# Tiles 6 to 15 of x loaded already turned, and centred by an accumulating DMA

## The chip, the cores and the metric

The kernel runs on one core of one Trainium2 chip. Its engines are TensorE (PE; its weight loads are listed as PEld), VectorE (DVE), ScalarE (ACT), GpSimd (POOL) and SyncE (SP). SP, ACT and POOL also issue DMA transfers, and each issues its own in the order of its queue. The metric is device time in microseconds; the kernel before was timed three times, and the median counts.

## The reference

All arrays are fp32. x has 2048 rows of 512. The two branches, a linear attention with 32 heads of 16 and a gated MLP of width 1376, both read the layer-normalised x.

```python
xn = _layernorm(x, axis=-1)                       # (x - mean) / sqrt(var + 1e-5)
return x + _A_ref(xn, wqkv, w_phi, wo) + _B_ref(xn, w_in, w_sp, b_sp, w_out)

# A: q, k, v = split(xn @ wqkv);  phi(t) = [softmax(t @ w_phi), softmax(-t @ w_phi)] per head
#    kv = phi_k^T v;  z = sum_s phi_k;  o = (phi_q kv) / (phi_q z + 1e-6);  A = o @ wo
# B: z = gelu(xn @ w_in);  z1, z2 = halves of z;  z2 = layernorm(z2)
#    g = w_sp @ z2 + b_sp;  B = (z1 * g) @ w_out
```

## The kernel before

The 2048 rows are cut into 16 tiles of 128 rows (`NT`), the 512 columns into 4 chunks of 128 (`ND`). Each matmul is made of three in fp32r, with operands cut into a rounded high part and a rest (`mm3`, lines 54 to 57): high by high, high by low, low by high. The high part is written by ACT (`round_h`, L47), the rest by VectorE (`rest_l`, L51).

There are three stages. The first, up to about 210 us, goes over the 16 tiles of x and makes q, k, v, their softmaxes, the sum of k and v, and the first half of the MLP's input product. The second makes the second half, and the third, the longest, the product with `w_sp` by a scheme of seven products; at its end the outputs are put together.

The change is in the first stage. TensorE contracts over partitions, so it needs x with its columns on partitions, x^T. For each tile s, `centered(s)` does this, called two tiles ahead, at step s - 2 of the loop in line 451:

- SP loads the rows, 256 KB (`load_x`, L179); five buffers (`XB`) hold them.
- VectorE makes mean and variance (`stats`, L260 and L261); POOL makes the negative mean (`neg_mean`, L265), and 1 / sqrt(var + eps) (L92, L93), which is applied later, to the outputs of the projections.
- ACT adds the negative mean to each row, in place (`center`, L269).
- TensorE turns the tile by four matmuls with the identity into one PSUM buffer (`transposed`, L275). Four such buffers (tag `mm`) are shared with the projections of q, k and v.
- ACT and VectorE split the PSUM buffer into high part and rest (`split_x`, L47 and L51) in a tile of the pool `xz`. That is x^T of the tile, named `xT` in the profile, kept for all later products.

A step s of the loop then fetches the rows of tile s + 4, projects k and makes its pair of softmaxes (`softmax_pair`: L111, L112, L117 and L118 on VectorE, the exponential L119 on ACT, the sums L122 and reciprocals L123 on VectorE), calls `centered(s + 2)`, projects some q, whose softmaxes go to DRAM (`e_d`, a POOL transfer), adds the normalised k softmaxes into `zacc` by an accumulating POOL transfer (`add_kv`, L307 and L308) and multiplies them with v in batches (L319), projects v of tile s + 1, and makes z1 of older tiles (`z1_raw`, L149).

The pool `xz` has 16 buffers. Before the x^T tiles need them all, they hold raw weights, and six of these (`spare`, line 449) serve as the softmax tiles of steps 2, 3, 4, 5, 8 and 9.

The order on each engine isn't the order of the text: a planner simulates the kernel by its own costs, and each engine's instructions are written out in the order in which they became ready there, earlier text first. `tc.issue_after(ins)` puts the instructions of its block behind `ins` on the engine of `ins`. Once it is written out, the order on each engine and queue is fixed, and an instruction that waits holds up all that stand behind it.

Of the kernel before, what the change touches and what calls it, by code (L numbers as in the profile page):

```python
# [10 lines left out]
F32 = mybir.dt.float32  # L11
F32R = mybir.dt.float32r
AF = mybir.ActivationFunctionType
ALU = mybir.AluOpType
# [4 lines left out]
P = 128  # L19
S, D, H, DH, FH = 2048, 512, 32, 16, 688  # L20
NT = S // P
ND = D // P
FC = FH // 2
NG = 4
NF = 2 * D
# [4 lines left out]
EPS_LN = 1e-5  # L30
EPS_DEN = 1e-6
XB = 5
NP = NT // 2
HP, QP = P // 2, P // 4
FP = 3 * P
# [4 lines left out]
def mixer(ctx: ExitStack, tc: tile.TileContext, x, x_t, wv, wqkT, phi_bd, wo, w_in, wst, b_r, w_out, out):  # L40
    nc = tc.nc
    pe, act, dve, pool, sp = nc.tensor, nc.scalar, nc.vector, nc.gpsimd, nc.sync


    def round_h(eng, h, src):
        if eng is act:
            return act.activation(h, src, AF.Copy).ins  # L47
        return eng.tensor_copy(h, src).ins

    def rest_l(l, src, h, eng=None):  # L50
        return (eng or dve).tensor_tensor(l, src, h.bitcast(F32), op=ALU.subtract).ins  # L51
# [18 lines left out]
    def xz_tile(n, dt, name):  # L70
        return xz.tile([P, SL], dt, tag="xz", name=name)[:, :n]

    mid = ctx.enter_context(ExitStack())
    dram = ctx.enter_context(tc.tile_pool(name="dram", bufs=1, space=DRAM))
# [2 lines left out]
    u_d = dram.tile([NT, FU, P], F32, name="u_d")  # L77
    kvT_d = dram.tile([P, D], F32, name="kvT_d")
    zb_d = dram.tile([P, NF], F32, name="zb_d")

    ident = cst.tile([P, P], F32, name="ident")
    make_identity(nc, ident)
# [3 lines left out]
    mv_x = cst.tile([P, NT, 2], F32, name="mv_x")  # L86
    r_x = cst.tile([P, NT], F32, name="r_x")

    def rstd_of(mv, r, stats=None):
        if stats is not None:  # L90
            dve.bn_aggr(mv, stats)
        pool.tensor_scalar_add(mv[:, 1:2], mv[:, 1:2], EPS_LN)  # L92
        pool.tensor_tensor(r, mv[:, 1:2], mhalf, op=ALU.pow)  # L93

    def heads(ap):
        return ap.rearrange("p (h d) -> p h d", d=DH)
# [8 lines left out]
    def bc(ap, n):  # L105
        return ap.unsqueeze(2).to_broadcast([P, n, DH])

    def softmax_pair(pl, src, tag, scale=1.0, ebufs=2, meanwhile=lambda: None, er=None):

        mm = pl.tile([P, 2, H], F32, tag=tag + "mm", bufs=1, name="mm")  # L110
        dve.tensor_reduce(mm[:, 0], heads(src), axis=AX.X, op=ALU.max)  # L111
        dve.tensor_reduce(mm[:, 1], heads(src), axis=AX.X, op=ALU.min)  # L112
        if er is None:
            er = pl.tile([P, NF + 2 * H], F32, tag=tag + "e", bufs=ebufs, name="e")
        e, r = er[:, :NF], er[:, NF:]
        e2 = e.rearrange("p (h a d) -> p h a d", a=2, d=DH)
        dve.tensor_tensor(e2[:, :, 0], heads(src), bc(mm[:, 0], H), op=ALU.subtract)  # L117
        dve.tensor_tensor(e2[:, :, 1], bc(mm[:, 1], H), heads(src), op=ALU.subtract)  # L118
        act.activation(e, e, AF.Exp, scale=scale)  # L119
        meanwhile()  # L120
        sm = pl.tile([P, 2 * H], F32, tag=tag + "sm", bufs=1, name="sm")
        dve.tensor_reduce(sm, heads(e), axis=AX.X, op=ALU.add)  # L122
        dve.reciprocal(r, sm)  # L123
        return er
# [47 lines left out]
    with ExitStack() as p0:  # L172
        res = p0.enter_context(left("p0res", 1))
        wk = p0.enter_context(left("p0wk", 2))
        ps = p0.enter_context(psum("p0ps", 4))

        def load_x(s):
            t = wk.tile([P, D], F32, tag="x", bufs=XB, name="xt")
            sp.dma_start(t, x[s * P:(s + 1) * P, :])  # L179
            return t  # L180
# [5 lines left out]
        def stage(name, dt=F32):  # L186
            return xz_tile(2 * FH, dt, name).rearrange("p (a b) -> p a b", a=2)
# [6 lines left out]
        bd_t = stage("bd")  # L194
# [50 lines left out]
        xt, v, rounded, ready = {}, {}, [], []  # L245

        def fetch(s):
            if s < NT:
                xt[s] = load_x(s)

        def split_x(src):
            t = xz_tile(2 * D, F32R, "xT").rearrange("p (a b) -> p a b", a=2)
            xT.append(t)
            src = src.rearrange("p a b -> p (a b)")
            rounded.append(round_h(act, t[:, 0], src))
            return rounded[-1], rest_l(t[:, 1], src, t[:, 0])

        def stats(s, keep=lambda **ins: None):
            st6 = wk.tile([P, 6], F32, tag="st6", name="st6")
            dve.bn_stats(st6, xt[s])  # L260
            keep(dve=dve.bn_aggr(mv_x[:, s], st6).ins)  # L261

        def neg_mean(s):
            nm = wk.tile([P, 1], F32, tag="nm", name="nm")
            pool.tensor_scalar_mul(nm, mv_x[:, s, 0:1], -1.0)  # L265
            return nm

        def center(s, nm):
            return act.activation(xt[s], xt[s], AF.Identity, bias=nm).ins  # L269

        def transposed(s):
            xs = xt.pop(s)
            pt = ps.tile([P, ND, P], F32, tag="mm", name="pt")
            for c in range(ND):
                ins = pe.transpose(pt[:, c], xs[:, c * P:(c + 1) * P], ident).ins  # L275
            return pt, ins

        def centered(s):
            stats(s)
            nm = neg_mean(s)  # L280
            rstd_of(mv_x[:, s], r_x[:, s:s + 1])
            with tc.issue_after(rounded[s - 2]):
                center(s, nm)
            split_x(transposed(s)[0])

        def keep_v(s, p):
            v[s] = wk.tile([P, D], F32, tag="v", bufs=4, name="v")
# [6 lines left out]
        spare = {}  # L294

        def proj_k(s):
            er = spare[s].rearrange("p a b -> p (a b)")[:, :NF + 2 * H] if s in spare else None
            return softmax_pair(wk, proj(s, wqk_h[:, 1], wqk_l[:, 1]), "k", r_x[:, s:s + 1], er=er)

        def proj_q(s):  # L300
# [28 lines left out]
        wkT_t = load_rows.raw  # L329
        fetch(2)  # L330
        wqT = load_rows(wqkT[:D])
        wqT_t = load_rows.raw
        fetch(3)
        w1r = [stage("w1row") for _ in range(2)]
# [5 lines left out]
        def keep(**ins):  # L340
            for i in ins.values():
                queue.enter_context(tc.issue_after(i))
# [6 lines left out]
            keep(pe=i)  # L349

        queue = ExitStack()
        tbl = wk.tile([P, 1], F32, tag="nm", name="tbl")
        keep(act=act.activation(tbl, mhalf, AF.Identity, bias=mhalf).ins)
        warm_up(7)
        stats(0, keep)
# [4 lines left out]
        nm = neg_mean(1)  # L360
# [17 lines left out]
        t = xz_tile(2 * D, F32R, "xT").rearrange("p (a b) -> p a b", a=2)  # L378
# [8 lines left out]
        for cs, pt in zip(halves, pts):  # L387
            src = pt.rearrange("p a b -> p (a b)")
# [8 lines left out]
        p = ps.tile([P, D], F32, tag="mm", name="proj")  # L397
        proj(0, wv_h, wv_l, p, (0, 1, 2))
        keep(pe=proj.last)
        pt = turned(1)  # L400
# [4 lines left out]
        p = ps.tile([P, D], F32, tag="mm", name="proj")  # L405
# [12 lines left out]
        nm = settled(2)  # L418
# [4 lines left out]
        nm = settled(3)  # L423
        p = ps.tile([P, D], F32, tag="mm", name="proj")
        proj(0, wqk_h[:, 1], wqk_l[:, 1], p, (0, 1))
        keep(pe=proj.last)
        pt = turned(2)
# [18 lines left out]
        split_x(turned(3))  # L446
        z1_raw(wk, za, 0, 2)
        keep(pe=zproj.last)
        spare.update(zip((2, 3, 4, 5, 8, 9), [bd_t] + wkT_t + wqT_t[:1] + w1r))
        n1, nq = 1, 0  # L450
        for s in range(NT):
            fetch(s + 4)
            er = ek[s] if s < len(ek) else proj_k(s)
            if 1 < s < NT - 2:
                centered(s + 2)
            while nq < (s - 2) * NT // (NT - 3):
                proj_q(nq)
                nq += 1
            add_kv(s, er)
            if s == 0:  # L460
                tiles = fold_tiles(((za, "z"), (ps, "mm")))
                keep(pe=fold(0, wqT, tiles))
                folded(0, tiles)
            elif s == 1:
                proj_v(3)
            elif 2 < s < NT - 1:
                proj_v(s + 1)
            while n1 < s * (NT - LAG) // (NT - 1):
                z1_raw(wk, za, n1, 2)
                n1 += 1  # L470
            if s == 3:
                queue.close()
# [33 lines left out]
    NQ = NT // QC  # L506
    NC = NP * NQ


    SEQ = [(i, q) for i in range(NP) for q in (range(NQ) if i < NP - 1 else (1, 2, 3, 0))]  # L510

# [40 lines left out]
    with ExitStack() as p1:  # L552
# [44 lines left out]
        for s in range(NE):  # L597
            et = load_q(s, tb.tile([P, QW], F32, name="et") if s else tmp1.tile([P, 4, D], F32, tag="zhl", name="et").rearrange("p a b -> p (a b)")[:, :QW])
            tmp = zw.tile([P, 4, FC], F32, tag="z2", bufs=2, name="qtmp").rearrange("p a b -> p (a b)")[:, :NF]
            e, _ = q_fin(et, tmp, zb)  # L600
# [57 lines left out]
    for s in range(NT):  # L658
        p = zproj((kv_ps_p, zc, zbp, za)[s % 4], s, w2, (0, 1) if s % 2 == 0 else (1, 0))
# [7 lines left out]
        for k, q in p:  # L667
            ins = act.activation(z[:, k], q, AF.Gelu_apprx_tanh, scale=r_x[:, s:s + 1]).ins
# [67 lines left out]
    def gate(i, cb, z, u, ut, after=None):  # L736
# [10 lines left out]
        def turn():  # L747
# [3 lines left out]
            for b in range(0, P, BL):  # L751
                (pool if i == NP - 2 else sp).dma_start(dst[:, :, b:b + BL], src[b:b + BL].rearrange("p (m b) -> p m b", b=BL))

# [49 lines left out]
    for n in range(NC):  # L803
        i = SEQ[n][0]
        if n % NQ == 1 and i < NP - 1:
            z = load_z1(i)
        products(n, g)
        if n % NQ == NQ - 1 and i < NP - 1:
            c = gt.tile([P, 2, FU], F32, tag="c", name="c")
# [5 lines left out]
        if n + 2 < NC:  # L815
            A[n + 2] = prep_a(n + 2, raw.pop(n + 2))
        if n % NQ == NQ - 1 and i < NP - 1:
            turn = gate(i, cb, z, c, z, prep_a.last)
# [12 lines left out]
        if n == NC - 2:  # L831
            es[0], es[1] = first_q(0), first_q(1)
            t = xz_tile((KF + 1) * P, F32R, "u1")
# [10 lines left out]
    wk = ctx.enter_context(left("cwk", 2))  # L844
# [125 lines left out]
    p, nxt = {}, dict(enumerate(uT))  # L970
# [61 lines left out]
```

## Time and profile before

| | |
|---|---|
| Three runs | 627.75, 628.66, 630.17 us; median 628.66 us |
| The profiled execution | 627.78 us |
| Its span, first to last instruction | 626.1 us |
| Granted TensorE clock | 0.999 |
| Transposes of x tiles after the first | 60, mean 272 ns |
| Centring passes on ACT | 15, median 712 ns |
| Statistics passes on VectorE | 16, median 688 ns |
| Busy, of the span | PE 99%, PEld 90%, DVE 81%, ACT 45%, POOL 17% |
| DMA | 98.40 MB, mean 157 GB/s |

A row of the profile names engine, line of the kernel, operation, and what is written from what (`pt<-ident,xt` writes `pt` from `ident` and `xt`); then how many, the busy microseconds and the mean duration in nanoseconds, or minimum, median and maximum. In a timeline the first column is the start and the second how long the row's instructions took together. A row of waits says who waited for whom: microseconds in total, how often, and the longest. Matmuls overlap, so the sum of their durations is more than the time that they take.

### The profile page before, as it was taken

To read this page: it belongs to the slowest core of one execution; us is meant where nothing else is said; L and a number is where in the kernel's file an instruction comes from. 1 tells how busy PE (TensorE), PEld (TensorE's weight loads), DVE (VectorE), ACT (ScalarE), POOL (GpSimd) and SP (SyncE) were. 2 spreads that over 40 slices of the span, in tenths; PEclk is the share of its full clock that TensorE was granted. 3 is DMA by queue.
4 is the path that set the end of the run, shared out by engine and by line. 5 is a ranking of instruction groups with operands and counts; after the bars stand their busy time and mean duration, and the time that the engine had idled before them with its cause. 6 is when DMAs were issued, how large, how long until landed. Compare 5 with 4: busy or idle time off the path is not lost.

```text
span 626.1 us, 11429 instructions
## 1 busy us (share of the span) xinstructions
PE 619.1 (99%) x4406; PEld 565.3 (90%) x4406; DVE 508.8 (81%) x893; ACT 280.7 (45%) x446; POOL 104.8 (17%) x187
## 2 busy tenths in 40 slices
PE   8999999999999999999999999999999999999996
PEld 7888888888888999999999999999999877788775
DVE  5999998987988398989898897696978899989211
ACT  5653434443333367877434444243445433334331
POOL 4142122111011015442000000000000212211110
PEclk9999999999999999999999999999999999999999
DMA  9445465354336868001454845637367799984722
GB/s 313 164 109 144 121 156 155 88 143 136 104 93 173 274 234 285 2 2 35 147 115 147 193 96 153 136 119 175 88 174 232 224 297 330 320 249 97 180 34 51
DMA packets 87590, 98.40 MB, mean 157 GB/s; under 512 B 46560, under 2 KB 59616, under 8 KB 87296
## 3 DMA queue, kind: packets, MB, share of 16 engines
q1 hardware_dynamic: 75200, 58.12, 32.4%
q0 software_dynamic: 10032, 33.92, 20.7%
q10 hardware_dynamic: 2304, 5.64, 2.4%
q8 instruction: 34, 0.56, 0.4%
q14 instruction: 20, 0.16, 0.1%
HBM read 56.37 MB, written 30.54 MB: 139 GB/s over the span
## 4 chain that ended last, share of the span: by engine, by line
PE 98%; DVE 0%; ACT 0%; POOL 0%; issue 0%; DVEq 0%; POOLq 0%
PE g L57 11%; PE g L56 11%; PE g L55 11%; PE proj L57 7%; PE proj L55 7%; PE proj L56 7%; PE zps L57 6%; PE zps L55 6%; PE zps L56 6%; PE pout L55 5%; PE pout L57 5%; PE pout L56 5%; PE ptq L890 1%; PE po L905 1%; PE kvps L319 1%; PE pout L919 1%
## 5 line engine op out<-in xcount | busy, mean ns | idle before, releaser
L56 PE MATMUL g<-B,A 128*128 128x344 f32 x448 | 143.3, 320 | 0.0
L55 PE MATMUL g<-B,A 128*128 128x344 f32 x448 | 142.8, 319 | 0.0
L57 PE MATMUL g<-B,A 128*128 128x344 f32 x448 | 140.6, 321 | 0.1
L55 PEld LDWEIGHTS g<-B,A 128*128 128x128 f32 x448 | 84.3, 188 | 0.0
L56 PEld LDWEIGHTS g<-B,A 128*128 128x128 f32 x448 | 84.2, 188 | 0.0
L57 PEld LDWEIGHTS g<-B,A 128*128 128x128 f32 x448 | 83.6, 188 | 0.4 <-DVE A L51 0.4
L47 ACT ACTIVATE A<-S 128x512 fp32r<-128x512 f32 x64 | 39.4, 630 | 71.3 <-DVE S L542 51.3
L55 PE MATMUL proj<-wqk_h,xT 128*128 128x512 f32 x128 | 50.6, 395 | 0.0
L57 PE MATMUL proj<-wqk_h,xT 128*128 128x512 f32 x128 | 50.2, 393 | 0.0
L56 PE MATMUL proj<-wqk_l,xT 128*128 128x512 f32 x128 | 49.9, 390 | 0.0
L47 ACT ACTIVATE A<-wf 128x512 fp32r<-128x512 f32 (+1 forms) x64 | 33.2, 521 | 36.3 <-DMA wf<-in_wst 14.3
L119 ACT ACTIVATE e<-e,r_x 128x1024 f32<-128x1024 f32 x26 | 29.9, 1150 | 40.2 <-DVE e L118 39.6
L51 DVE TENSOR_TENSOR A<-S,A 128x512 fp32r<-128x512 f32 x64 | 43.1, 686 | 4.8 <-ACT A L47 4.3
L55 PE MATMUL zps<-w_0h,xT 128*128 128x344 f32 x128 | 41.4, 323 | 0.0
L57 PE MATMUL zps<-w_0h,xT 128*128 128x344 f32 x128 | 41.0, 320 | 0.0
L55 PE MATMUL zps<-w_1h,xT 128*128 128x344 f32 x128 | 40.9, 320 | 0.0
L57 PE MATMUL zps<-w_1h,xT 128*128 128x344 f32 x128 | 40.7, 319 | 0.0
L56 PE MATMUL zps<-w_0l,xT 128*128 128x344 f32 x128 | 40.6, 317 | 0.0
L56 PE MATMUL zps<-w_1l,xT 128*128 128x344 f32 x128 | 40.6, 317 | 0.0
L51 DVE TENSOR_TENSOR A<-wf,A 128x512 fp32r<-128x512 f32 (+1 forms) x64 | 35.0, 549 | 2.6 <-ACT A L47 2.4
L707 POOL DMA_DIRECT2D z1t<-z_d x16 | 8.7, 547 | 165.5 <-DMA u_d<-z1t 98.7
L122 DVE TENSOR_REDUCE sm<-e 128x64 f32<-128x1024 f32 x26 | 31.4, 1207 | 5.1 <-ACT e L119 5.0
(205 smaller groups left out, 1432.7 us busy)
## 6 DMA issues: line engine op xcount, KB each, us to landing
wf<-in_wst SPq DMA_DIRECT2D x64, 256.0 KB, 3.4
e_d<-e POOLq DMA_DIRECT2D x16, 544.0 KB, 4.6
et<-e_d SPq DMA_DIRECT2D x16, 544.0 KB, 6.4
er<-et POOLq DMA_DIRECT2D x12, 512.0 KB, 6.4
z_d<-z1f ACTq DMA_DIRECT2D x16, 344.0 KB, 2.6
z1t<-z_d POOLq DMA_DIRECT2D x16, 344.0 KB, 5.2
zacc<-e POOLq DMA_DIRECT2D x10, 512.0 KB, 4.7
u<-u_d SPq DMA_DIRECT2D x15, 320.0 KB, 5.6
```

The source lines that it names most:

```text
L47: return act.activation(h, src, AF.Copy).ins
L51: return (eng or dve).tensor_tensor(l, src, h.bitcast(F32), op=ALU.subtract).ins
L55: pe.matmul(dst, ah, bh, start=start, stop=False)
L56: pe.matmul(dst, ah, bl, start=False, stop=False)
L57: return pe.matmul(dst, al, bh, start=False, stop=stop).ins
L119: act.activation(e, e, AF.Exp, scale=scale)
L122: dve.tensor_reduce(sm, heads(e), axis=AX.X, op=ALU.add)
L319: i = pe.matmul(kv_acc[k:k + QP, m // 4], vs[:, m * QP:(m + 1) * QP], e[:, m * HP:(m + 1) * HP], start=first and m < 4 and len(ready) == n ...
L707: pool.dma_start(t[:, k, :FH], z1_d[2 * i + k])
L890: pe.transpose(pt[:, a, k].bitcast(F32R), src, ident_r)
L905: lasts[3] = pe.matmul(po[r][c * QP:(c + 1) * QP, k], kvT[rows, m // 2, cols], fs[m // 4][rows, m // 2 % 2], start=True, stop=True).ins
L919: lasts[2] = pe.matmul(p, rt, w, start=False, stop=i == NT - 1 and k == 1).ins
```

## The change

From tile 6 on (`FT`), x^T no longer comes from TensorE. The kernel already had `x_t` among its inputs, x with each tile turned, and did not use it. Now:

- `fetch` still loads the rows of each tile, as before up to tile 5, and six steps ahead from tile 6 on, for the statistics alone.
- `lay_x(s)`, four steps ahead, loads the turned tile, again 256 KB, on SP. Tiles 6 to 12 lie two by two in buffers of `xz`, tiles 13 to 15 (`LT`) in the buffers of the row tiles.
- `send_mean(s)`, four steps ahead and on VectorE behind the last split, makes the statistics, the negative mean on POOL and 1 / sqrt(var + eps), and SP stores the negative means to DRAM (`nm_d`), four copies of 128 numbers, each number a piece of its own.
- `center_t(s)`, three steps ahead and on POOL's queue behind the next tile's negative mean, is one POOL transfer that adds these 512 numbers to each of the 128 rows of the turned tile.
- `split_x` reads the turned tile from SBUF, behind the step's k softmax differences on VectorE and its exponential on ACT.

The four transposes and the centring pass of tiles 6 to 15 are gone. Steps 8 and 9 take fresh buffers of `xz` for their softmax tiles in place of raw weight tiles. The small tiles `nm` have four buffers in place of two.

```diff
+FT, LT = 6, 13
+    nm_d = dram.tile([NT, ND, P], F32, name="nm_d")
-        dve.tensor_tensor(e2[:, :, 1], bc(mm[:, 1], H), heads(src), op=ALU.subtract)
-        act.activation(e, e, AF.Exp, scale=scale)
+        less = dve.tensor_tensor(e2[:, :, 1], bc(mm[:, 1], H), heads(src), op=ALU.subtract).ins
+        softmax_pair.last = less, act.activation(e, e, AF.Exp, scale=scale).ins
...
-            nm = wk.tile([P, 1], F32, tag="nm", name="nm")
+            nm = wk.tile([P, 1], F32, tag="nm", bufs=4, name="nm")
...
+        lay = {}
+        def lay_x(s):
+            if s >= LT:
+                xc = wk.tile([P, D], F32, tag="x", bufs=XB, name="xt")
+            elif (s - FT) % 2 == 0:
+                lay_x.pair = xz_tile(2 * D, F32, "xc")
+                xc = lay_x.pair[:, :D]
+            else:
+                xc = lay_x.pair[:, D:]
+            sp.dma_start(xc, x_t[s].rearrange("p c t -> p (c t)"))
+            lay[s] = xc
+        def send_mean(s):
+            with tc.issue_after(split_x.last):
+                stats(s)
+            xt.pop(s)
+            nm = wk.tile([P, 1], F32, tag="nm", bufs=4, name="nmt")
+            send_mean.last = pool.tensor_scalar_mul(nm, mv_x[:, s, 0:1], -1.0).ins
+            sp.dma_start(nm_d[s].rearrange("c t -> t c"), nm.to_broadcast([P, ND]))
+            rstd_of(mv_x[:, s], r_x[:, s:s + 1])
+        def center_t(s):
+            with tc.issue_after(send_mean.last):
+                pool.dma_start(lay[s], nm_d[s].rearrange("c t -> (c t)").unsqueeze(0).to_broadcast([P, D]), accum_op=ALU.add)
...
-            er = spare[s].rearrange("p a b -> p (a b)")[:, :NF + 2 * H] if s in spare else None
+            er = (spare[s] or stage("er")).rearrange("p a b -> p (a b)")[:, :NF + 2 * H] if s in spare else None
...
-        spare.update(zip((2, 3, 4, 5, 8, 9), [bd_t] + wkT_t + wqT_t[:1] + w1r))
+        spare.update(zip((2, 3, 4, 5, 8, 9), [bd_t] + wkT_t + wqT_t[:1] + [None] * 2))
...
-            fetch(s + 4)
+            if s + 4 < FT:
+                fetch(s + 4)
+            if FT <= s + 6 < NT:
+                fetch(s + 6)
+            if FT <= s + 4 < NT:
+                lay_x(s + 4)
             er = ek[s] if s < len(ek) else proj_k(s)
-            if 1 < s < NT - 2:
+            if 1 < s < FT - 2:
                 centered(s + 2)
+            elif FT - 2 <= s < NT - 2:
+                with tc.issue_after(softmax_pair.last[0]), tc.issue_after(softmax_pair.last[1]):
+                    split_x(lay.pop(s + 2))
+            if FT <= s + 4 < NT:
+                send_mean(s + 4)
+            if FT <= s + 3 < NT:
+                center_t(s + 3)
```

More of the change, by code (lines that the diff above doesn't have):

```diff
@@ L253, in split_x @@
             xT.append(t)
-            src = src.rearrange("p a b -> p (a b)")
             rounded.append(round_h(act, t[:, 0], src))
-            return rounded[-1], rest_l(t[:, 1], src, t[:, 0])
+            split_x.last = rest_l(t[:, 1], src, t[:, 0])
+            return rounded[-1], split_x.last
         def stats(s, keep=lambda **ins: None):
@@ L275, in transposed @@
                 ins = pe.transpose(pt[:, c], xs[:, c * P:(c + 1) * P], ident).ins
-            return pt, ins
+            return pt.rearrange("p a b -> p (a b)"), ins
         def centered(s):
@@ L351, in mixer @@
         queue = ExitStack()
-        tbl = wk.tile([P, 1], F32, tag="nm", name="tbl")
+        tbl = wk.tile([P, 1], F32, tag="nm", bufs=4, name="tbl")
         keep(act=act.activation(tbl, mhalf, AF.Identity, bias=mhalf).ins)
```

## The prediction

> **What bounds the kernel now.** I read the page first, its busy shares and its chain of waits, then the waits of TensorE alone.
>
> ```profile
> span 626.1 us, 11429 instructions
> ...
> PE 619.1 (99%) x4406; PEld 565.3 (90%) x4406; DVE 508.8 (81%) x893; ACT 280.7 (45%) x446; POOL 104.8 (17%) x187
> ...
> PE 98%; DVE 0%; ACT 0%; POOL 0%; issue 0%; DVEq 0%; POOLq 0%
> ```
> ```profile
> PE idle L348 <- POOL ident masks.py:199: 1.8, 1, 1.8
> ```
>
> The chain that ends last is TensorE from one end to the other, and TensorE waited once in the whole span: 1.8 us for the identity at the start. So the time is the sum of what TensorE is given, and a microsecond taken from its stream comes off the end, if nothing else becomes late. The edit lies in the first stage, the loop over the 16 tiles. There the second thing to read is VectorE, by stretches of 20 us (the columns are the stretch, its length, then busy time and count of PE, weight loads, DVE, ACT and POOL).
>
> ```profile
> 45.00:65.00 20.00, 20.00 (x216) 17.06 (x216) 19.81 (x32) 6.92 (x9) 5.93 (x12) 1.00 0.46 115
> 65.00:85.00 20.00, 20.00 (x104) 17.39 (x103) 18.75 (x31) 9.79 (x13) 4.50 (x10) 1.00 0.57 153
> 85.00:105.00 20.00, 20.00 (x105) 17.48 (x105) 18.35 (x28) 7.87 (x11) 4.03 (x7) 1.00 0.42 117
> 105.00:125.00 20.00, 20.00 (x216) 16.95 (x215) 18.01 (x28) 8.23 (x12) 3.42 (x7) 1.00 0.48 137
> 125.00:145.00 20.00, 20.00 (x102) 17.23 (x101) 17.77 (x26) 8.15 (x11) 2.85 (x4) 1.00 0.51 144
> ```
>
> TensorE is full in every stretch; VectorE is full up to 65 us (19.81 of 20) and has 1.25 to 2.2 us left in each later one. ACT and POOL have more than half their time free. VectorE is therefore the engine that the change must not load.
>
> **What is removed, and its price.** Tiles 6 to 15 lose four transposes each, 40 in all, and one centring pass each on ACT. A transpose's own duration says little, because matmuls overlap; the price is read from starts. Around the transposes of tile 9:
>
> ```profile
> 88.08 0.40 PE L57 MATMUL proj<-wqk_h,xT 128*128 128x512 f32 x1
> 88.31 0.60 PE L275 MATMUL pt<-ident,xt 128*128 128x128 f32 x4
> 88.67 0.48 PE L55 MATMUL proj<-wqk_h,xT 128*128 128x512 f32 x1
> ...
> 91.28 0.39 PE L57 MATMUL proj<-wqk_h,xT 128*128 128x512 f32 x1
> ...
> 94.00 0.39 PE L57 MATMUL proj<-wqk_h,xT 128*128 128x512 f32 x1
> ```
>
> From 88.08 to 91.28 lie twelve projection matmuls and the four transposes: 3.20 us. From 91.28 to 94.00 lie twelve of the same matmuls alone: 2.72 us. The four transposes cost 3.20 - 2.72 = 0.48 us: 0.36 from their first start to the next matmul's, and 0.12 in matmuls spaced wider behind them. Ten tiles give 4.8 us. The lower bound takes the 0.36 alone, 3.6 us; the upper takes the whole 0.60 for which the group is shown busy, 6.0 us. I take 4.8, since it is a difference of two equal pieces of work.
>
> The Trainium skill (TensorE: Matmul & The Clock Gate, Part 4: PE-mode transpose) gives some 275 ns for a transpose in one kernel's context. An estimate that adds this up 40 times would be 11.0 us, a median of 617.7. The starts above contradict the adding: four of them pass in 0.36 us here, so the page's figure is a latency and not a cost.
>
> **What ACT and VectorE do per tile.** ACT loses its centring (0.71 us each, 7.1 us in all, of an engine under half busy: worth nothing to the end). The split into high and low part now reads SBUF where it read PSUM:
>
> ```profile
> L269 ACT ACTIVATE xt<-xt,nm x15: 707/712/724, 8.7 to 140.0; 128x512 f32<-128x512 f32 x15
> L51 DVE TENSOR_TENSOR xT<-pt,xT x17: 417/681/693, 6.1 to 167.4; 128x512 fp32r<-128x512 f32 x15, 128x256 fp32r<-128x256 f32 x2
> L51 DVE TENSOR_TENSOR A<-S,A 128x512 fp32r<-128x512 f32 x64 | 43.1, 686 | 4.8 <-ACT A L47 4.3
> ```
>
> The last row is the same subtraction from SBUF in the third stage: 686 ns against 681, no difference. The statistics (one pass and a small one) stay, but move. Now they run as soon as a row tile has landed; in the changed kernel those of tile s+4 stand behind the split of tile s+2.
>
> ```profile
> 31.03 1.22 DVE L260 BATCH_NORM_STATS2 st<-xt 128x6 f32<-128x512 f32 x2
> ...
> 58.46 0.69 DVE L260 BATCH_NORM_STATS2 st<-xt 128x6 f32<-128x512 f32 x1
> ```
> ```profile
> L261 DVE BATCH_NORM_AGGREGATE mv_x<-st 128x2 f32<-128x6 f32 x6 | 1.0, 166 | 0.0
> ```
>
> Counting the passes from the first tile on, the two at 31.03 are tiles 6 and 7 and the one at 58.46 is tile 11. Behind the splits, 66 us sees only tile 8 done. So three passes of 0.69 + 0.17 = 0.86 us, 2.6 us, leave the stretch in which VectorE is full and go into the stretch from 65 to 145. There VectorE has 18.75 + 18.35 + 18.01 + 17.77 = 72.9 us; with them 75.5. TensorE's 80 us shrink by seven tiles to 80 - 7 x 0.48 = 76.6. VectorE still fits, by 1.1 us, and it enters the stretch 2.6 us less late than now. Also the transposed tile no longer takes one of the four PSUM buffers that the projections share, which gives TensorE more room when VectorE is late. I cost the move at nothing; the cover is thin, and without it the first rival comes.
>
> **What is added.** Per tile: a second load of 256 KB on SP, POOL's small product with -1 (in place of the one before), a store of the negative means on SP (512 single numbers), and one accumulating transfer from POOL, 256 KB. No accumulating transfer from DRAM into SBUF is in the trace. The nearest rows are the sums into `zacc`, same queue and stage, 512 KB, and the stores of `e_d`; for the scattered store, `u_d`, which goes in 128-byte pieces.
>
> ```profile
> L308 POOL DMA_DIRECT2D zacc<-e x10: 864/878/1072, 34.0 to 199.9; - x10
> DMA to landing us min/median/max: 4.5/4.6/6.7
> ```
> ```profile
> DMA to landing us min/median/max: 2.8/5.1/10.7
> ```
> ```profile
> u_d<-z1t SPq DMA_DIRECT2D x24, 184.0 KB, 4.4
> xt<-in_x SPq DMA_DIRECT2D x16, 256.0 KB, 3.9
> ```
>
> The first landing row is that of `zacc`, the second that of `e_d`, its reloads among them. I take 4.6 us for the centring transfer, bounded by 2.8 and 10.7. The load has a step and more (the tiles' distance, 12.5 us, worked out below) for its 3.9 us, and the store one step for its 4.4. POOL spends 0.88 us on issuing each centring, 9 us in all, against a load of 4 us in 20. Queued behind SP's wait for the means are only later loads, which are asked for two steps ahead; behind POOL's wait stand the next `zacc` and `e_d` transfers. What is tight is the way from one split to the next (rows of POOL's product, of the split of tile 7 on VectorE, of that of tile 8 on ACT):
>
> ```profile
> L265 POOL TENSOR_SCALAR nm<-mv_x x15: 210/239/250, 6.0 to 117.9; 128x1 f32<-128x1 f32 x15
> ```
> ```profile
> 68.58 0.68 DVE L51 TENSOR_TENSOR xT<-pt,xT 128x512 fp32r<-128x512 f32 x1
> ```
> ```profile
> 76.61 0.60 ACT L47 ACTIVATE xT<-pt 128x512 fp32r<-128x512 f32 x1 [1.45 <-PE pt L275]
> ```
>
> The split of tile 7 ends at 69.26; then come the statistics (0.86), POOL's product (0.24, taken as 0.3 with its start) and, behind it, the transfer that centres tile 8: it starts at about 70.6 and lands at 75.2. ACT now begins tile 8's split at 76.61. It fits by 1.4 us, in the tightest of the steps that I followed. So the added work lies beside TensorE, and its cost is 0.
>
> **Sum.** 626.1 - 4.8 = 621.3 us of span; the profiled execution took 627.78, 1.7 us more than its span, so 623.0. The median of the runs, 628.66, lies 0.9 above that execution: 623.9. By the bounds 3.6 and 6.0: 625.1 and 622.7.
>
> **Rivals.** First, VectorE becomes the pace in the stretch from 65 to 145 us. Its idle time there is 80 - 72.9 = 7.1 us; the waits of VectorE between 45 and 145 us name most of it:
>
> ```profile
> DVE st L260 <- DMA xt<-in_x: 2.6, 2, 1.9
> DVE sm L122 <- ACT e L119: 2.3, 3, 1.2
> ```
>
> The 2.6 for row tiles goes, as these are fetched a step or two earlier. If the other 4.5 stays as it is, VectorE needs 75.5 + 4.5 = 80.0 us, the stretch stays 80 long, and only the three tiles outside it (6, 14, 15) pay: 3 x 0.48 = 1.4, 627.2 us. For it: the 1.1 us margin, and an order that the planner writes out anew and that may fit the chip less well. Against: TensorE never waited for VectorE, even where that was busy 19.81 of 20.
>
> Second, slower: centring is a loop. A tile's transfer is issued behind the statistics of a tile that stand behind the split of the tile before, and its landing releases the next split. Bare, the loop is 0.86 + 0.3 + landing + 0.60 + 0.68. The step that it must fit is the distance of the transposes:
>
> ```profile
> 52.78 0.60 PE L275 MATMUL pt<-ident,xt 128*128 128x128 f32 x4
> ...
> 165.43 0.60 PE L275 MATMUL pt<-ident,xt 128*128 128x128 f32 x4
> ```
>
> Tiles 6 to 15, nine steps: 112.65 / 9 = 12.5 us, 12.0 after the change. It decides from a landing of 12.0 - 2.4 = 9.6 us on. At the 10.7 of the slowest `e_d` transfer it costs 1.1 x 9 = 9.9 us and the gain is 4.8: 633.8 us. For it: a kind of transfer that the trace lacks, behind others on one queue. Against: twice the landing of every near row.
>
> Third, a port that VectorE and POOL share. The split's subtraction will have both inputs in SBUF, as that of `add_kv` on L307 has; a POOL instruction that reads SBUF could hold it up for at most its own length.
>
> ```profile
> L93 POOL TENSOR_TENSOR r_x<-mv_x,mhalf x7: 568/571/578, 46.0 to 110.8; 128x1 f32<-128x1 f32 x7
> ```
> ```profile
> L307 DVE TENSOR_TENSOR e<-e x3: 1208/1217/1218, 87.0 to 135.5; 128x1024 f32<-128x1024 f32 x3
> ```
>
> At 0.57 for seven tiles, 4.0 us more than the first rival's 80.0, less the 1.4 outside: 631.3 us. The product of L307 shows no such delay, within 10 ns of itself. The Trainium skill (SBUF — State Buffer, Who interferes with whom) states this rule: a VectorE instruction with two SBUF inputs contends with GpSimd's reads, and the second to start waits for the whole of the first. The trace bears it out nowhere.
>
> That the change does not do what it says could only mean that the 40 transposes are still in the stream; the diff leaves no call to them from tile 6 on.
>
> **Chances.** Forecast 0.62, first rival 0.22, second 0.12, third 0.04. About 0.5%, 3.1 us, is what a measurement here can tell from none; the forecast with its bounds is beyond it, the first and the third rival within. Faster 0.62, within 0.26, slower 0.12. The forecast's own range is 622.7 to 625.1; the range of 8 in 10 takes in the first rival and the spread of the runs on either side: 622.3 to 630.0.
>
> **What would show it.** In the changed profile L275 has 20 transposes and not 60; TensorE's only wait is again that for the identity; the two transposes on either side of a missing group are gone without wider spacing, and the span is 621.3. Each centring lands under 7 us, and ACT does not wait for one over 2 us. VectorE from 65 to 145 us is busy over nine tenths. Waits of TensorE for VectorE or ACT would show the first rival, waits of ACT's split for the centring transfer at every tile the second, subtractions of the split over 1 us the third. Wrong outright would be a span above 624.5 with none of these waits.

## The result

The changed kernel is slower. Six runs lie between 663.79 and 669.49 us, median 666.0, against 629.6 for the kernel before in the same comparison: a ratio of 1.0573, 95% interval 1.053 to 1.0616. The profiled execution took 669.49 us, with a span of 667.7, against 627.78 and 626.1.

The changed kernel's page, its busy shares, its granted clock in 40 slices and its chain of waits:

```profile
PE 630.2 (94%) x4366; PEld 570.8 (85%) x4366; DVE 507.7 (76%) x893; ACT 271.6 (41%) x436; POOL 119.9 (18%) x197
...
PEclk9999997699789999999999999999999997999999
...
PE 68%; DMA 11%; issue 11%; DVE 6%; POOL 2%; ACT 1%; SPq 0%; POOLq 0%; DVEq 0%; ACTq 0%
```

TensorE no longer carries the chain alone: 11% of it are DMA transfers. TensorE's idle time is 667.7 - 630.2 = 37.5 us, where it was 626.1 - 619.1 = 7.0. It is also busy for 11.1 us more, although it has 40 transposes less, because its granted clock drops with its waits. 30.5 + 11.1 = 41.6 us, the whole difference of the spans. Of the 30.5 us of added idle time, 27.0 lie in the first 225 us (TensorE is busy for 196.09 of them, before for 223.09). By stretches (columns as in the prediction; the last three are the granted clock, the share of the DMA engines and GB/s):

```profile
65.00:85.00 20.00, 19.04 (x96) 16.33 (x95) 14.51 (x25) 4.52 (x6) 8.04 (x12) 1.00 0.77 159
85.00:105.00 20.00, 19.11 (x94) 16.28 (x93) 15.23 (x24) 4.85 (x6) 4.75 (x7) 1.00 0.65 112
105.00:125.00 20.00, 9.32 (x119) 6.76 (x117) 10.89 (x17) 4.83 (x6) 4.89 (x7) 0.66 0.71 130
...
165.00:185.00 20.00, 11.44 (x162) 10.35 (x164) 13.96 (x22) 5.41 (x7) 5.20 (x8) 0.80 0.74 99
185.00:205.00 20.00, 15.31 (x76) 12.16 (x68) 9.13 (x15) 3.40 (x4) 3.01 (x5) 0.86 0.34 96
```

In the stretch from 105 us no engine is full: TensorE does 9.32 of 20 us at a clock of 0.66, and VectorE, which was my concern, 10.89. The engines wait for something else. TensorE's waits, then the waits of the other engines, then the transfers with their median time to landing:

```profile
PE proj L56 <- DVE e L120: 9.4, 3, 4.7
PE kvps L350 <- DVE e L338: 8.6, 1, 8.6
PE zps L56 <- ACT z1f L151: 6.0, 2, 4.6
```
```profile
ACT xT L48 <- DMA xc<-nm_d: 35.0, 6, 7.3
...
DVE e L119 <- DMA zacc<-e: 11.9, 2, 9.7
...
DVE e L119 <- DMA e_d<-e: 8.0, 3, 5.6
```
```profile
e_d<-e POOLq DMA_DIRECT2D x16, 544.0 KB, 9.7
...
xc<-in_x_t SPq DMA_DIRECT2D x7, 256.0 KB, 10.5
xc<-nm_d POOLq DMA_DIRECT2D x7, 256.0 KB, 8.7
...
nm_d<-nmt SPq DMA_DIRECT2D x10, 2.0 KB, 9.7
```

TensorE waits mostly for the softmaxes (L120 and L338), and for ACT's z1; VectorE's softmax L119 waits for buffers that `e_d` and `zacc` transfers have not yet read; ACT's split waits for the centring. The transfers are late: the store of 2 KB of means takes 9.7 us, as long as a transfer of 544 KB, and `e_d`, which the edit does not touch, went from a median of 4.6 us to 9.7.

### The profile page after: what moved, and what is told of

The parts are those of the page before. It is cut to its first block, busy times and chain, and to the rows that moved or that the text cites. A ratio compares the mean times of both kernels' runs of the same rounds, so it can differ in the third digit from the quotient of the medians.

```text
span 667.7 us, 11409 instructions
## 1 busy us (share of the span) xinstructions
PE 630.2 (94%) x4366; PEld 570.8 (85%) x4366; DVE 507.7 (76%) x893; ACT 271.6 (41%) x436; POOL 119.9 (18%) x197
## 4 chain that ended last, share of the span: by engine, by line
PE 68%; DMA 11%; issue 11%; DVE 6%; POOL 2%; ACT 1%; SPq 0%; POOLq 0%; DVEq 0%; ACTq 0%
PE g L58 11%; PE g L57 10%; PE g L56 10%; PE pout L56 5%; PE pout L58 5%; PE pout L57 4%; PE zps L56 4%; PE zps L58 4%; PE zps L57 4%; DMA xc<-nm_d 3%; DMA nm_d<-nmt 2%; DMA zacc<-e 2%; DMA et<-e_d 2%; DVE sm L124 2%; DMA e_d<-e 1%
## 5 line engine op out<-in xcount | busy, mean ns | idle before, releaser
L56 PE MATMUL proj<-wqk_h,xT 128*128 128x512 f32 x128 | 52.0, 406 | 5.6 <-DVE e L120 5.6
L58 PE MATMUL proj<-wqk_h,xT 128*128 128x512 f32 x128 | 51.4, 402 | 0.0
L57 PE MATMUL proj<-wqk_l,xT 128*128 128x512 f32 x128 | 51.4, 401 | 0.0
L56 PEld LDWEIGHTS proj<-wqk_h,xT 128*128 128x128 f32 x128 | 25.0, 196 | 11.1 <-issue 5.1
```

Of the source, the lines that this page charges most:

```text
L56: pe.matmul(dst, ah, bh, start=start, stop=False)
L57: pe.matmul(dst, ah, bl, start=False, stop=False)
L58: return pe.matmul(dst, al, bh, start=False, stop=stop).ins
```

## The experiments

All but the last keep the written-out orders of the changed kernel on TensorE, VectorE and ACT, instruction by instruction. Only the last one's differ a little. Where x is not centred, as each expectation says, the work on TensorE is the same.

**Store and centring, one without the other.** The four edits of the changed kernel:

```diff
 # no store; the centring adds row 0 of wv
-            sp.dma_start(nm_d[s].rearrange("c t -> t c"), nm.to_broadcast([P, ND]))
...
-                pool.dma_start(lay[s], nm_d[s].rearrange("c t -> (c t)").unsqueeze(0).to_broadcast([P, D]), accum_op=ALU.add)
+                pool.dma_start(lay[s], wv[0:1, :].to_broadcast([P, D]), accum_op=ALU.add)
 # no centring: the last line above goes, the store stays
 # neither: both lines go
 # own rows: no store, and the centring adds x[s * P:(s + 1) * P, :]
```

> The changed kernel without the store of the negative means; the centring transfer stays, with the same shape, and adds row 0 of wv (one stretch of 2 KB read for all 128 rows) in place of the negative means, so x isn't centred. The orders on TensorE, VectorE and ACT are those of the changed kernel. Theory A (the store of 512 single numbers is slow to land and holds up the transfers beside it): the centring lands in 4 to 5.5 us instead of 8.7, TensorE hardly waits, the time is 623 to 628 us. Theory B (the centring transfer itself is slow, since 128 rows read the same 2 KB): it still lands in 8 us or more and the time stays above 650 us. Theory C (the second load, or the new order of the engines, costs the time): 655 to 668 us.

> The changed kernel without the centring transfer: the means are stored, but x isn't centred. Same orders on TensorE, VectorE and ACT. Theory A: ACT no longer waits for a late tile, but the stores still hold up the e_d and zacc transfers, which land in 8 us or more as in the changed kernel (9.7 and 6.2); 626 to 640 us. Theory B: with the slow transfer gone, 623 to 627 us and e_d and zacc land in about 4.6 us, as before the change. Theory C: 655 to 668 us.

> The changed kernel with neither the store nor the centring transfer: turned tiles are loaded and split, x isn't centred. Same orders on TensorE, VectorE and ACT. Theories A and B: the 40 transposes are all that is left of the change, so 4.8 us under the kernel before, 623 to 626 us, and TensorE waits only for the identity. Theory C: 650 us or more.

> As the kernel without the store, but the centring transfer adds 128 different rows of 2 KB (the tile's own rows of x) in place of one stretch read 128 times; x isn't centred. Theory A: the same time as without the store, within 2 us, since what is read doesn't matter. Theory B: the transfer lands 2 us or more sooner than with the one stretch and the time falls by 10 us or more against that kernel.

| | median us | ratio to before, 95% interval |
|---|---|---|
| no store | 624.48 | 0.9933 (0.9912 to 0.9955) |
| no centring | 653.68 (643.13 to 655.33) | no interval, its runs lie too far apart |
| neither | 624.88 | 0.9943 (0.9928 to 0.9957) |
| own rows | 624.26 | 0.9936 (0.9919 to 0.9952) |

Theory A holds. With the store gone, everything else in place, the time is below that of the kernel before. The profile without the store, TensorE's waits, the centring's landing and the stretch from 65 to 145 us:

```profile
PE idle L378 <- POOL ident masks.py:199: 1.8, 1, 1.8
```
```profile
xc<-in_wv POOLq DMA_DIRECT2D x7, 256.0 KB, 4.2
```
```profile
65.00:145.00 80.00, 80.00 (x511) 69.32 (x510) 76.90 (x122) 28.91 (x37) 30.55 (x44) 1.00 0.67 176
```

TensorE waits for the identity alone, and the centring, still one stretch read for 128 rows, lands in 4.2 us. Reading 128 different rows changes nothing (624.26), so theory B falls. Theory C falls too: these kernels have the second load and the new orders. VectorE is busy for 76.90 of 80 us and delays nobody.

The store alone, with no centring to wait for, costs 653.68 - 624.88 = 28.8 us by the medians. Its size is uncertain: three of the four runs took 653.31 to 655.33 us, one 643.13, and that one still lies 18.3 above. All are over the 626 to 640 us expected under theory A. The waits and transfers of the run of 653.31 us, the last two rows from two stretches of it, 55 to 185 us and 190 to 240 us:

```profile
DVE e L119 <- DMA e_d<-e: 24.9, 4, 9.8
...
PE proj L56 <- DVE e L120: 12.6, 2, 11.5
```
```profile
e_d<-e POOLq DMA_DIRECT2D x16, 544.0 KB, 10.1
...
xc<-in_x_t SPq DMA_DIRECT2D x7, 256.0 KB, 10.5
zacc<-wrow POOLq DMA_DIRECT2D x3, 512.0 KB, 10.6
...
nm_d<-nmt SPq DMA_DIRECT2D x10, 2.0 KB, 10.1
```
```profile
e_d<-e POOLq DMA_DIRECT2D x11, 544.0 KB, 10.9
```
```profile
e_d<-e POOLq DMA_DIRECT2D x5, 544.0 KB, 4.6
```

Nothing in this kernel reads what is stored. The loss comes from the transfers beside the store: `e_d` lands in 10.1 us, VectorE waits 24.9 us for buffers that it holds, and TensorE waits for VectorE. The last store is issued at 169.9 us, and from 190 us on `e_d` is back at 4.6. The changed kernel is about another 12 us slower (666.0 against 653.68, medians of two comparisons), with the split waiting for a centring that is late in the same way.

**What is slow about the store.** Three things could be: 512 pieces, their 4 bytes, or that they lie side by side. In the kernel without centring:

```diff
-    nm_d = dram.tile([NT, ND, P], F32, name="nm_d")
+    nm_d = dram.tile([NT, ND, P, 16], F32, name="nm_d")
 # spread: 4 bytes, 64 bytes apart
+            sp.dma_start(nm_d[s, :, :, 0].rearrange("c t -> t c"), nm.to_broadcast([P, ND]))
 # wide: 64 bytes, 64 bytes apart
+            sp.dma_start(nm_d[s].rearrange("c t w -> t c w"), ident[:, :ND * 16].rearrange("p (c w) -> p c w", w=16))
```

> As the kernel with the store alone (no centring transfer, x isn't centred), but each of the 512 numbers goes to a place of its own in DRAM, 64 bytes from the next, in place of 4 bytes. Theory A1 (many small writes into the same short stretch of DRAM follow one another there): the store lands in under 6 us where it took 10.1, nothing beside it is held up, the time is 623 to 628 us. Theory A2 (each write of 4 bytes is slow by itself, wherever it goes): it lands in 8 us or more and the time stays at 640 to 656 us. Theory A3 (the count of 512 pieces is what costs): as A2.

> As the kernel with the store alone and its numbers 64 bytes apart, but each of the 512 pieces is 64 bytes long (the store writes columns of the identity; x isn't centred). Theory A1: as the spread store, 623 to 628 us. Theory A2: the store lands in under 6 us and the time is 623 to 628 us, while the spread store stays slow. Theory A3: 640 to 656 us, since there are still 512 pieces.

Spread: 625.66 us, ratio 0.9948 (0.993 to 0.9965). Wide: 625.25 us, 0.9947 (0.993 to 0.9965). The spread store's transfers, then the issue of the wide one, with its first and last start in us:

```profile
e_d<-e POOLq DMA_DIRECT2D x16, 544.0 KB, 5.4
...
xc<-in_x_t SPq DMA_DIRECT2D x7, 256.0 KB, 3.9
zacc<-wrow POOLq DMA_DIRECT2D x3, 512.0 KB, 4.6
...
nm_d<-nmt SPq DMA_DIRECT2D x10, 2.0 KB, 2.5
```
```profile
L309 SPq DMA_DIRECT2D nm_d<-ident x10: 360/505/1870, 15.4 to 25.7; - x10
```

The same 512 writes of 4 bytes land in 2.5 us, and `e_d` is back at 5.4, as in the kernel with neither. Neither count nor size is enough to cause the delay; that the pieces lie side by side is what differs. The wide run can't add to this: its stores read the identity and not the means, so all were issued by 25.7 us, before the first `e_d`. So the distance was varied, with the last dimension of `nm_d` at 8, 4 and 2 numbers:

> The store alone again (no centring transfer, x isn't centred), the 512 numbers 32 bytes apart: 4 bytes apart landed in 10.1 us, 64 bytes apart in 2.5. If what is shared is a stretch of 64 bytes and each write in it waits for the one before, two in each stretch add one wait: the store lands in 3 to 4 us (10.1 - 2.5 = 7.6 us for 15 further writes, 0.5 each) and the time is 624 to 628 us. If what is shared is longer, 512 bytes (128 writes at 4 bytes apart, 16 at 32, 8 at 64, those not seen to cost), also 3 us. If any sharing of a 64-byte stretch brings the whole hold-up: 8 us or more and over 640 us.

> As before, 16 bytes apart, four in each 64 bytes. By one wait of 0.5 us for each further write: 4 us of landing, 624 to 630 us. By any sharing: 8 us or more, over 640 us.

> As before, 8 bytes apart, eight in each 64 bytes. By one wait of 0.5 us for each further write: 6 us of landing, 626 to 640 us. By any sharing: 8 us or more, over 640 us.

The store's row at 8, at 16 and at 32 bytes apart:

```profile
nm_d<-nmt SPq DMA_DIRECT2D x10, 2.0 KB, 4.7
```
```profile
nm_d<-nmt SPq DMA_DIRECT2D x10, 2.0 KB, 3.3
```
```profile
nm_d<-nmt SPq DMA_DIRECT2D x10, 2.0 KB, 2.7
```

| bytes apart | landing us | over 64 apart | time us | ratio to before |
|---|---|---|---|---|
| 4 | 10.1 | 7.6 | 653.68 | none |
| 8 | 4.7 | 2.2 | 625.35 | 0.9935 (0.9906 to 0.9963) |
| 16 | 3.3 | 0.8 | 625.86 | 0.9946 (0.9918 to 0.9973) |
| 32 | 2.7 | 0.2 | 624.3 | 0.9921 (0.9891 to 0.9952) |
| 64 | 2.5 | 0 | 625.66 | 0.9948 (0.993 to 0.9965) |

Each halving of the distance about triples the excess or more. That is steeper than the 0.5 us for each further write that the expectations took, by which the three stores would have landed later than they did, and it isn't all or nothing. The stretch that a store fills grew with the distance, from 2 KB to 32, and its length was not varied alone. At 8 bytes the excess has no effect on the time; at 4 it has the whole.

**Fewer pieces, just as close.** The 128 means are stored once, and the centring reads the copy four times for each row.

```diff
-            sp.dma_start(nm_d[s].rearrange("c t -> t c"), nm.to_broadcast([P, ND]))
+            sp.dma_start(nm_d[s, 0:1].rearrange("c t -> t c"), nm)
-                pool.dma_start(lay[s], nm_d[s].rearrange("c t -> (c t)").unsqueeze(0).to_broadcast([P, D]), accum_op=ALU.add)
+                pool.dma_start(lay[s].rearrange("p (c t) -> p c t", c=ND), nm_d[s, 0].unsqueeze(0).unsqueeze(0).to_broadcast([P, ND, P]), accum_op=ALU.add)
```

> The changed kernel whole, but the store writes the 128 negative means once, not four times, and the centring transfer reads the one copy four times for each row (512 pieces of 512 bytes in place of 128 of 2 KB). If the hold-up goes with the number of 4-byte writes, it is a quarter: the store lands in some 5 us where it took 9.7, the centring in 5 to 6, and the time is 624 to 632 us. If a store of any 4-byte writes has a fixed price, it lands in 8 us or more and the time stays above 645 us.

674.73 us, ratio 1.0731 (1.0702 to 1.0761): slower still than the changed kernel, and the expectation of a quarter of the hold-up was wrong. Its store's row:

```profile
nm_d<-nmt SPq DMA_DIRECT2D x10, 0.5 KB, 8.3
```

A quarter of the pieces, at the same distance, lands in 8.3 us, so fewer pieces are no cure. The edit also cuts the centring into pieces of 512 bytes (a median of 10.3 us for the first seven). What that does to the store and to the time was not taken apart.

**A store of whole stretches.** The means are turned on VectorE first:

```diff
-    nm_d = dram.tile([NT, ND, P], F32, name="nm_d")
+    nm_d = dram.tile([NT, BL, P], F32, name="nm_d")
+    means = mask[:, P:].rearrange("p (k b) -> p k b", b=BL)
     mask = mask[:, :P]
...
-            nm = wk.tile([P, 1], F32, tag="nm", bufs=4, name="nmt")
-            send_mean.last = pool.tensor_scalar_mul(nm, mv_x[:, s, 0:1], -1.0).ins
-            sp.dma_start(nm_d[s].rearrange("c t -> t c"), nm.to_broadcast([P, ND]))
+            nm, row = means[:, s % 2], means[:, 2 + s % 2]
+            dve.tensor_scalar_mul(nm, mv_x[:, s, 0:1].to_broadcast([P, BL]), -1.0)
+            dve.transpose(row, nm)
+            sp.dma_start(nm_d[s].rearrange("j (q i) -> q j i", i=BL), row)
...
-            with tc.issue_after(send_mean.last):
-                pool.dma_start(lay[s], nm_d[s].rearrange("c t -> (c t)").unsqueeze(0).to_broadcast([P, D]), accum_op=ALU.add)
+            pool.dma_start(lay[s], nm_d[s, :ND].rearrange("c t -> (c t)").unsqueeze(0).to_broadcast([P, D]), accum_op=ALU.add)
```

> The changed kernel whole, with the means turned before they are stored: VectorE writes the negative mean 32 times beside itself and turns blocks of 32 by 32, so each partition holds 32 means of its block in a row, and one store writes 128 pieces of 128 bytes (32 copies, of which the centring transfer reads four as one stretch of 2 KB). Two small VectorE instructions per tile are added, POOL's product goes. If the scattered store was the whole of the loss: the store lands in 3 to 5 us, TensorE waits only for the identity, and the time is 623 to 626 us, under the kernel before by what the 40 transposes cost. If the orders of the engines (which move a little) or the chain from means to split still bind: 627 to 640 us.

623.43 us, ratio 0.9916 (0.9902 to 0.9931): nothing of the computation is left out, and it beats both kernels, the one before by 5.2 us, or 0.8%. Its busy shares, its centring's landing, and its split on VectorE:

```profile
PE 614.2 (99%) x4366; PEld 560.4 (90%) x4366; DVE 508.2 (82%) x913; ACT 271.3 (44%) x436; POOL 117.5 (19%) x187
```
```profile
xc<-nm_d POOLq DMA_DIRECT2D x7, 256.0 KB, 5.5
```
```profile
L52 DVE TENSOR_TENSOR xT<-xc,xT x7: 679/681/685, 62.4 to 132.1; 128x512 fp32r<-128x512 f32 x7
```

TensorE is full again, 4.9 us less busy than before the change. Here too the means go through DRAM and are added by an accumulating transfer, one step ahead. What differs is the shape of the store, and where the means are made.

## Why the prediction was wrong

The forecast of 623.9 us and the range up to 630.0 missed 666.0, on the other side.

- **The removed transposes: right in size, a little high.** 4.8 us was the price, 3.6 to 6.0 the bounds. Against the median of before in their comparison, the kernels in which TensorE hardly waits gained 3.4 (neither), 3.8 (no store), 4.0 (own rows), 5.2 (whole stretches) and, with the stores 8 to 64 bytes apart, 2.5 to 4.0 us. Several lie under the lower bound. Comparing two equal pieces of the timeline gave far the better size than the 11.0 us of adding up durations. The changed profile has 4366 instructions on TensorE, 40 fewer than the 4406 before, so the change does what it says.
- **VectorE and the moved statistics: right, close.** 75.5 us of work from 65 to 145 us were forecast, 76.90 is what the kernel without the store shows, and TensorE did not wait. The first rival isn't what happened.
- **The port that VectorE and POOL share: no effect on the time, but it is in the trace.** The changed kernel's splits of turned tiles took 681 to 693 ns, as those from PSUM did, so the third rival's delay did not come. No POOL calculation ran beside such a split, so they don't test the rule. Where the two did meet, POOL was the one that waited:

```profile
81.01 1.19 DVE L338 TENSOR_TENSOR wrow<-wrow 128x1024 f32<-128x1024 f32 x1
81.19 1.11 POOL L308 TENSOR_SCALAR nmt<-mv_x 128x1 f32<-128x1 f32 x1 [9.27 <-DVE mv_x L263]
```
```profile
L308 POOL TENSOR_SCALAR nmt<-mv_x x10: 238/1105/1111, 41.9 to 179.6; 128x1 f32<-128x1 f32 x10
```

  POOL's product, "0.24, taken as 0.3 with its start", took 1.10 us or more in seven of ten tiles, each time beside the product of `add_kv`, which has both inputs in SBUF, and ended just behind it. The trace of the kernel before has such a case too, at 38.20 us (1.10 in place of 0.21), so "the trace bears it out nowhere" was a misreading. It does not explain the loss: without the store the products are as long (239/1106/1111), and the time is 624.48.
- **The centring transfer: right by itself.** 4.6 us was taken; without the store it lands in 4.2. In the changed kernel it lands in 8.7.
- **The store: the step that failed.** The prediction gave it "one step for its 4.4", from the row of `u_d`, whose pieces are 128 bytes long, and went on to "the added work lies beside TensorE, and its cost is 0". It landed in 9.7 us. Unlike the centring transfer's, its landing was given no bounds. Worse, I asked only whether the store itself would land in time. It mostly did. POOL's one wait for a store in the changed kernel:

```profile
POOL xc L315 <- DMA nm_d<-nmt: 2.3, 1, 2.3
```

  That it would delay the transfers beside it was in no term of the sum: 28.8 us by the medians, and 18.3 by the fastest run, come with the store alone, in a kernel in which nobody waits for it.
- **The second rival had the sign and the symptom, not the cause.** ACT's split does wait for the centring, 35.0 us in six waits, and by the same loop. But the rival asked for a landing above 9.6 us of a slow kind of transfer, and put 633.8 us on it. The kind of transfer isn't slow (4.2 without the store). In the changed kernel its median of 8.7 is below that point, though single ones, issued at 135.0 and 164.7 us, took 10.9 and 11.1. By the medians the larger part of the loss comes without the loop.
- **The clock was left out.** TensorE is busy for 11.1 us more than before and for 15.6 more than in the kernel without the store (614.6), which gives it the same work: it works at a lower granted clock after its waits. A stall in a kernel that TensorE fills costs more than its length.

## What to carry to other kernels

A column with one number on each partition, stored to DRAM as a row of neighbouring numbers, is a small transfer that can hold up those beside it for microseconds: turn it on an engine first. Leaving room between the numbers also cured the store, but was tried only where nothing reads them back. When a transfer of a new shape is added, price what it does to the transfers beside it, and not only whether it arrives in time; the nearest row must match in the length of its pieces and in how they lie, not in bytes. Where TensorE sets the end, a transposition saved is worth what two equal pieces of the timeline differ by, not its duration.

## What the runs showed that I had not expected

Neighbouring 4-byte writes are dear by their distance: 10.1 us of landing at 4 bytes apart, 4.7 at 8, 3.3 at 16, 2.7 at 32, 2.5 at 64, for the same 512 writes. While those at 4 bytes are under way, loads, stores and accumulating transfers on SP's and POOL's queues are late together (turned tiles 10.5 against 3.9 us, `e_d` 10.1 against 5.4, `zacc` from `wrow` 10.6 against 4.6). The Trainium skill (DMA: Bandwidth & Descriptors, Specifications) says that below 512 bytes a transfer is read, modified and written back. The runs agree only in part: at 64 bytes apart, pieces of 4 bytes cost nothing that shows in the time. Why close writes delay transfers that go elsewhere stays open.

The granted clock fell to 0.66 in the stretch from 105 to 125 us, in which TensorE was busy for 9.32 us, and was 1.00 in the stretches of this profile in which it was busy throughout. The Trainium skill (TensorE: Matmul & The Clock Gate, Part 1: The HAM clock gate) says that the array's clock is halved after an idle window of some 3.4 us and restored after a busy one; TensorE's waits here, up to 8.6 us, agree with that.
